# Attention, one-choice and two-choice expert layers in one launch on one core: hash rows finished in one step and moved by DMA, a cast moved to GpSimd, table fills laid out over the attention stage

## The chip, the cores and the metric

The kernel runs on one core of one Trainium2 chip. The metric is device microseconds of one execution. A core has five engines that run side by side, each with an instruction stream of its own, in order: PE (TensorE, matmul; its weight loads are shown as PEld), DVE (VectorE), ACT (ScalarE), POOL (GpSimd) and SP (SyncE), which here only issues DMAs. Sixteen DMA engines move the data. Whatever an engine waits for holds up everything behind it in its stream.

## The reference

```python
def reference(q, k, v, proj, moe, moe2):
    q_bits = einsum('bhsd,dk->bhsk', q, proj) > 0          # 6 bits a token
    k_bits = einsum('bhsd,dk->bhsk', k, proj) > 0
    mask = q_bucket[:, :, :, None] == k_bucket[:, :, None, :]   # all 6 bits equal
    scores = where(mask, q @ k.T / sqrt(64), -1e9)
    x = (softmax(scores) @ v)                              # 2 batches, 8 heads, 768 tokens, 64 wide
    x = x.transpose(0, 2, 1, 3).reshape(1536, 512)
    x = moe(x)     # the best of 8 experts a token, relu(x @ w1[e]) @ w2[e], times its weight
    return moe2(x) # the two best of 8 experts a token, noisy gate, the same kind of expert
```

## The kernel before

**Stages.** Attention comes first (to about 290 us), then the first expert layer (key 0 to 7), then the second (key 8 to 15). Attention has 16 heads (2 batches of 8) and works by groups: group g is half of head g // 2, so there are 32 groups of 384 queries. The two expert stages are planned apart from attention, in a second plan that the change does not touch.

**Precision.** Where f32 exactness is wanted, a value is split in a rounded high part and the rest (fp32r tiles: `hx` and `lx`, `eh` and `el`, two halves of `vh`), and matmuls are done on the parts.

**One head's preparation.** SP loads q and k of the head, turned, into `qk` (128 rows: 64 of q, 64 of k) and the values into `vr`. ACT rounds `qk` to `hx` (`prep_h`, L500); POOL subtracts to `lx` (`prep_l`, L544, four pieces). SP copies parts of `hx` and `lx` by DMA into `qa`, `ka`, `qb`, `kb` (`prep_hcopy` L508, four DMAs; `prep_lcopy` L548, two). `qa` and `ka` exist twice and alternate by head; `hx` has two buffers, so the rounding of head h waits until the DMAs that read `hx` of head h - 2 have landed.

**Hash rows.** PE projects `hx` and `lx` with the split `proj` (`bits_pe`, L567, into a PSUM tile `ET` of 108 rows, two pieces of 384 tokens). DVE makes the bits of it (`bits_sign`, L571): rows 64 to 75 of `qa` get the query's bits and the bits minus one, and rows 96 to 107 get the key's in the other order. Then the key's twelve rows are multiplied by 2^30 and moved down to rows 64 to 75 of `ka` (`bits_scale`): by DVE for heads 1 to 13 (L584, two pieces a head), by POOL for heads 14 and 15, by ACT for head 0 (`first_bits`, L538). Contracted together with the 64 rows of q and k they add minus 2^30 for each bit that differs, so the mask costs no pass of its own.

**One group.** PE makes three score pieces (`score_pe`, L597, four matmuls of 384 columns each, PSUM `S`, two buffers); DVE takes the row maximum (`score_max`, L602); POOL turns it into bias and scale, two small instructions (`score_scale`, L607 and L608); ACT takes the exponential into `es` (`score_exp`, L612). PE turns `es` in six blocks (`tr_pe`, L620, three transposes each, into `ET`, three buffers); ACT and DVE split each block (`tr_h` L624, `tr_l` L630); PE multiplies each block with the values, two matmuls (`pv`, L647 and L648, into `O`). The values' high part is a cast on DVE (`prep_vh`, L552), the low part two subtractions on POOL (`prep_vl`, L556). At a group's end ACT copies `O` out, PE turns it back (`fin_pe`, L657) and DVE scales it into `xrow` (`fin_out`, L671 and L673). So L671 runs once a group, and its start marks the end of that group.

**Order.** Each engine's order is made by a planner (`Plan`), from a cost and a due time for each step; `PR` is the table of due times. A planner's dependency only shapes the order: what an instruction really waits for on the chip follows from the data it reads and writes, and, for a DMA of SP, from the eighth DMA before it, which must have landed.

**Fills.** The gathered tables `xs1` and `xs2` and the output must hold a fill pattern before rows are scattered into them: 54 DMAs out of one row `zrow` (`init_x`, L454; with two small loads they are the list `inits`), some 260 KB each. SP issues them all in the first 135 us. After groups 14 and 15 the first six tiles of tokens are ranked, and POOL scatters their rows (`r1_scatter`, L719).

Of the kernel before, what the change touches and what calls it, by code (L numbers as in the profile page):

```python
# [9 lines left out]
F32 = mybir.dt.float32  # L10
F32R = mybir.dt.float32r
# [20 lines left out]
CB = float(2.0 ** 30)  # L32

# [4 lines left out]
PR = dict(sc=-7.0, mx=-7.5, ex=-5.5, pv=4.0, fin=7.0, bits=-16.0, prep=-26, load=-34.0, h=-1, l=0)  # L38
# [7 lines left out]
BSA, BSB, BSK, BSD, FSE = 1, 14, 2, .6, 0  # L46
BSE = lambda h: BSK if BSA <= h < BSB else 0
RA, K8, L1, L2 = 0, 7, 20, 1
WP, WR, WS = 4, 30, 2.5
LATE, ZP, Z2, L6, CR = 1, 23.0, 214.0, -4, 12  # L50
# [76 lines left out]
def fbits(t):  # L127
    return t.bitcast(F32)
# [3 lines left out]
def lsh_attention_moe_moe2_kernel(  # L132
# [251 lines left out]
    ld, wk, hl = ap("ld", 2), ap("wk", 2), ap("hl", 4)  # L384
# [26 lines left out]
    cbt = acon.tile([128, 192], F32, name="cbt")  # L411
    nc.gpsimd.memset(cbt[96:128], CB)

    def split_proj():
        nc.vector.tensor_copy(pst_h, pst)
        nc.vector.tensor_sub(pst_l, pst, pst_h)
# [119 lines left out]
    def first_bits(c):  # L536
        cs = slice(c * 384, c * 384 + 384)
        nc.scalar.activation(KA[0][64:76, cs], QA[0][96:108, cs], AF.Copy, scale=CB)  # L538
# [20 lines left out]
    BP = {}  # L559
# [9 lines left out]
    def bits_sign(h, c):  # L569
        cs = slice(c * 384, c * 384 + 384)  # L570
        nc.vector.tensor_scalar(QA[h % 2][64:108, cs], BP[h, c][64:108], 0.0, bsel[64:108],  # L571
                                op0=OP.is_gt, op1=OP.subtract)

    def bits_scale(h, c):
        s = h % 2
        if BSE(h) == 0:
            cs = slice(c * 192, c * 192 + 192)
            nc.gpsimd.tensor_tensor(KA[s][64:76, cs], QA[s][96:108, cs], cbt[96:108], op=OP.mult)
            return
        cs = slice(c * 384, c * 384 + 384)  # L580
# [7 lines left out]
    def score_pe(g, j):  # L588
        h, half = divmod(g, 2)
        s = h % 2  # L590
        if j == 0:
            SM[g] = wk.tile([128, 3], F32, name="sm", bufs=3)
        ES[g, j] = wk.tile([128, S], F32, name="es", bufs=8)
# [48 lines left out]
    def pv(g, kb):  # L642
        h = g // 2
        if kb == 0:
            OA[g] = psp.tile([128, 384], F32, name="O", bufs=1)
        w = VH[h][:, kb].rearrange("p a b -> p (a b)")
        nc.tensor.matmul(OA[g], w, EH[g, kb], start=kb == 0, stop=False)  # L647
        nc.tensor.matmul(OA[g], w, EL[g, kb], start=False, stop=kb == 5)  # L648
# [128 lines left out]
    plan = Plan(dict(S=2, ET=3, O=1, es=8, eh=4, el=4, ec=2, os=2, qk=3, vr=3, hx=2, lx=2, qb=2, vh=3,  # L777
# [8 lines left out]
    for h in range(HEADS):  # L786
        z = 12 * h
        due = lambda k, o=0.0: z + PR[k] + o
        if h > 1:
            add(("load", h), "SP", 1800, P(loads, h), due("load"), [("load", h - 1)] if h > 2 else [], lat=2200,  # L790
                new=[("qk", h), ("vr", h)])
# [27 lines left out]
        else:  # L819
            add(("ph", h), "ACT", 733, P(prep_h, h), due("prep"), ld_, use=[("qk", h)], new=[("hx", h)] + nq)  # L820
            add(("hc", h), "SP", 2500, P(prep_hcopy, h), due("prep", .1), [("ph", h)], lat=2200,
# [5 lines left out]
            add(("lc", h), "SP", 1250, P(prep_lcopy, h), due("prep", 1), [("pl", h, 3), ("hc", h)], lat=2200,  # L827
                use=[("lx", h), ("qb", h)])
            for c in range(2):
                add(("bp", h, c), "PE", 490, P(bits_pe, h, c), due("bits", 2 * c),  # L830
                    [("pl", h, 3), ("hc", h)], use=[("hx", h), ("lx", h)], new=[("ET", ("b", h, c))])
                add(("bt", h, c), "DVE", 525, P(bits_sign, h, c), due("bits", 2 * c + .5),
                    [("bp", h, c), ("hc", h)], use=[("ET", ("b", h, c)), ("qa", h)])
                for d in range(2):
                    if BSE(h) == 0:
                        add(("bs", h, 2 * c + d), "POOL", 552, P(bits_scale, h, 2 * c + d),
                            due("bits", 2 * c + .6 + .1 * d), [("bt", h, c)], use=[("qa", h)])
                    elif d == 0:
                        add(("bs", h, c), *(("ACT", 413) if BSE(h) == 1 else ("DVE", 269)), P(bits_scale, h, c),
                            due("bits", 2 * c + BSD), [("bt", h, c)], use=[("qa", h)])  # L840
        add(("vh", h), "DVE", 269, P(prep_vh, h), max(due("prep", 5), h - 5), ld_ + [("ph", h)] + FIRST[V0] * (h < 3) + [("at", 3 if h == 0 else 5)] * (h < 2), use=[("vr", h)],
# [5 lines left out]
    for g in range(NG):  # L847
        h = g // 2
        z = 6.0 * g
        for j in range(3):  # L850
            k, o = (g, j), 2 * j
            add(("sc",) + k, "PE", 650, P(score_pe, g, j), z + o + PR["sc"],
                ([("sc", g, j - 1)] if j else []) + (FIRST0[g] if h == 0 else [("hc", h)]) + [("lc", h)] + [("bt", h, c) for c in range(2)] + [("bs", h, c) for c in ((0, 3) if h == 0 else range(4) if BSE(h) == 0 else range(2))],
                use=[("qb", h), ("qa", h)] + ([("sm", g)] if j else []),
                new=[("S", k), ("es", k)] + ([] if j else [("sm", g)]))
            add(("mx",) + k, "DVE", 865, P(score_max, g, j), z + o + PR["mx"], [("sc",) + k], use=[("S", k)])
            add(("ms",) + k, *(("DVE", 135) if MS(g, j) else ("POOL", 330)), P(score_scale, g, j), z + o + PR["mx"] - 40, [("mx",) + k])
            add(("ex",) + k, "ACT", 971, P(score_exp, g, j), z + o + PR["ex"], [("ms",) + k],
                use=[("S", k), ("es", k), ("sm", g)])
        for kb in range(6):  # L860
            k = (g, kb)
            add(("tr",) + k, "PE", 330, P(tr_pe, g, kb), z + kb, [("ex", g, j) for j in range(3)] + [("c2",)],
                use=[("es", (g, j)) for j in range(3)], new=[("ET", k)])
            add(("th",) + k, "ACT", 371, P(tr_h, g, kb), z + kb + PR["h"], [("tr",) + k], use=[("ET", k)],
# [8 lines left out]
            else:  # L873
                add(("tl", 1) + k, "DVE", 469, P(tr_l, g, kb), z + kb + PR["l"], [("th",) + k],
                    use=[("ET", k), ("eh", k)], new=[("el", k)])
            add(("pv",) + k, "PE", 326, P(pv, g, kb), z + kb + PR["pv"],
                [("tl", 1) + k, ("vl", h, 1)] + ([("pv", g, kb - 1)] if kb else []),
                use=[("eh", k), ("el", k), ("vh", h)] + ([("O", g)] if kb else []), new=[] if kb else [("O", g)])
        add(("fa", g), "ACT", 371, P(fin_act, g), z + PR["fin"] - 1, [("pv", g, 5)], use=[("O", g)], new=[("os", g)])
        add(("fp", g), "PE", 598, P(fin_pe, g), z + PR["fin"], [("fa", g), ("ene",)], use=[("os", g)], new=[("ET", ("f", g))])  # L880
        add(("fs", g), *(("DVE", 70) if FSE else ("POOL", 190)), P(fin_eps, g), z + PR["fin"], [("ex", g, 2)], use=[("sm", g)])
        add(("fr", g), "DVE", 88, P(fin_rec, g), z + PR["fin"] - 1, [("fs", g)], use=[("sm", g)])
        add(("fo", g), "DVE", 363, P(fin_out, g), z + PR["fin"], [("fp", g), ("fr", g)],
            use=[("ET", ("f", g)), ("sm", g)])
    for k, f in enumerate(inits):
        add(("in", k), "SP", 900, f, 24 + 2.2 * k, [("in", k - 1)] if k else [("c3",), ("hc", 1)], lat=3000)
# [14 lines left out]
    for c in range(8):  # L901
        add(("wr", c), "SP", 1700, P(wload, c), (WR if c < WP else 150) + c, ([("in", 2)] if c < WP else [("in", len(inits) - 1)]) + ([("wl", c - 4, 7)] if c > 3 else []),
            lat=2500)
# [5 lines left out]
    for i, g in enumerate((14, 15, 30, 31)):  # L909
# [5 lines left out]
        for t in range(3):  # L915
            add(("rsa", T0, t), "ACT", 560, P(r1_sq, T0, t, 0), z - 3 + w * t, hot[:-1] + ([("rsa", T0, t - 1)] if t else []),
# [692 lines left out]
```

## Time and profile before

| what | value |
|---|---|
| three runs | 811.01, 807.99, 813.76 us, median 811.01 |
| the profiled execution: own time | 808.55 us |
| the profiled execution: span of its trace | 806.8 us |
| mean granted TensorE clock | 0.991 |
| PE busy | 774.3 us (96%) |
| DVE busy | 583.6 us (72%) |
| ACT busy | 479.5 us (59%) |
| POOL busy | 382.3 us (47%) |

The shares are averages over stages that have different limits. PE's busy time has matmuls that overlap: the duration of one is longer than the time from its start to the next one's. So pace is read from starts. Idle time of an engine stands in brackets, with what ended it.

### The profile page before, as it was taken

What the parts mean: (1) busy time and instruction counts of PE and PEld (TensorE: products, weight loads), DVE (VectorE), ACT (ScalarE), POOL (GpSimd) and SP (SyncE); (2) the same over time, 40 slices, a digit from 0 to 9 for tenths busy, and PEclk for the clock granted to TensorE, in tenths of its full rate; (3) what the DMA queues carried; (4) which work ended last, traced back from release to release, by engine and by line L of the source; (5) the groups of instructions that cost most, each with busy time, mean ns of one, the idle gap of its engine ahead of it and who ended that gap; (6) DMA issues with size and microseconds to landing.
All of it is one profiled execution on the core that took longest, in us unless ns stands there. A gap on an engine that the chain in (4) does not pass through costs nothing. (4 is left out here: it accounts for less than half of the span.)

```text
span 806.8 us, 14991 instructions
## 1 busy us (share of the span) xinstructions
PE 774.3 (96%) x5078; PEld 748.5 (93%) x5078; DVE 583.6 (72%) x1303; ACT 479.5 (59%) x1009; POOL 382.3 (47%) x669
## 2 busy tenths in 40 slices
PE   8999798998999999999999998999999999999995
PEld 6899787987999999999999998999999999999995
DVE  8999778999999868887787756684566475665511
ACT  6997777986888847556575544464353435354310
POOL 6655344557464260433123322108373745648474
PEclk9999989999999999999999999999999999999998
DMA  8999999664322158886677645765786776856332
GB/s 215 290 237 233 244 235 247 208 187 143 112 67 53 46 178 252 258 255 196 207 231 218 214 161 176 183 192 93 195 172 173 171 182 132 177 147 118 85 35 80
DMA packets 94076, 141.16 MB, mean 175 GB/s; under 512 B 26220, under 2 KB 58116, under 8 KB 93994
## 3 DMA queue, kind: packets, MB, share of 16 engines
q1 hardware_dynamic: 76730, 123.45, 55.2%
q0 software_dynamic: 17264, 16.70, 11.1%
q8 instruction: 42, 0.69, 0.4%
q14 instruction: 40, 0.33, 0.1%
HBM read 89.08 MB, written 36.06 MB: 155 GB/s over the span
## 5 line engine op out<-in xcount | busy, mean ns | idle before, releaser
L1264 POOL DMA_INDIRECT out_dram<-yo,idx x91 | 147.6, 1622 | 127.6 <-DVE yo L1261 102.0
L1056 PE MATMUL S<-xh,w0h 128*128 128x256 f32 (+1 forms) x512 | 165.0, 322 | 1.0 <-DVE hl L1066 1.0
L1057 PE MATMUL S<-xl,w0h 128*128 128x256 f32 (+1 forms) x512 | 161.4, 315 | 0.3 <-issue 0.3
L1058 PE MATMUL S<-xh,w0l 128*128 128x256 f32 (+1 forms) x512 | 161.7, 316 | 0.0
L1080 PE MATMUL ET<-hh,w1h 128*128 128x256 f32 (+2 forms) x504 | 158.5, 315 | 0.1
L1082 PE MATMUL ET<-hh,w1l 128*128 128x256 f32 (+2 forms) x504 | 158.2, 314 | 0.0
L1081 PE MATMUL ET<-hl,w1h 128*128 128x256 f32 (+2 forms) x504 | 157.8, 313 | 0.0
L1062 ACT ACTIVATE hh<-S 128x512 fp32r<-128x512 f32 (+1 forms) x64 | 46.8, 732 | 136.1 <-PE S L1058 130.1
L630 DVE TENSOR_TENSOR el<-ET,eh 128x384 fp32r<-128x384 f32 x192 | 102.0, 551 | 16.1 <-ACT eh L624 13.9
L612 ACT ACTIVATE es<-S,mxs 128x768 f32<-128x768 f32 x96 | 95.5, 995 | 15.7 <-POOL mxs L608 12.8
L620 PE MATMUL ET<-idf,es 128*128 128x128 f32 x576 | 92.1, 277 | 9.7 <-ACT es L612 7.1
L1066 DVE SCALAR_TENSOR_TENSOR hl<-S,hh 128x512 fp32r<-128x512 f32 (+1 forms) x64 | 54.5, 852 | 64.2 <-ACT hh L1062 62.3
L624 ACT ACTIVATE eh<-ET 128x384 fp32r<-128x384 f32 x192 | 89.7, 492 | 14.6 <-PE ET L620 11.3
L1056 PEld LDWEIGHTS S<-xh,w0h 128*128 128x128 f32 x512 | 96.3, 188 | 1.4 <-DVE hl L1066 1.2
L1057 PEld LDWEIGHTS S<-xl,w0h 128*128 128x128 f32 x512 | 96.4, 188 | 1.3 <-issue 0.5
L1058 PEld LDWEIGHTS S<-xh,w0l 128*128 128x128 f32 x512 | 96.2, 188 | 0.3
L1080 PEld LDWEIGHTS ET<-hh,w1h 128*128 128x128 f32 x504 | 94.9, 188 | 1.1 <-ACT ys L1104 0.7
L1081 PEld LDWEIGHTS ET<-hl,w1h 128*128 128x128 f32 x504 | 94.8, 188 | 0.7
L602 DVE TENSOR_REDUCE mxs<-S 128x1 f32<-128x768 f32 x96 | 91.5, 953 | 5.1 <-PE S L597 4.0
L1082 PEld LDWEIGHTS ET<-hh,w1l 128*128 128x128 f32 x504 | 94.7, 188 | 0.3
L620 PEld LDWEIGHTS ET<-idf,es 128*128 128x128 f32 x576 | 71.9, 142 | 20.6 <-ACT es L612 8.1
L217 DVE TENSOR_TENSOR w1l<-wraw,w1h 128x512 fp32r<-128x512 f32 x128 | 81.9, 681 | 11.8 <-ACT w1h L211 11.8
(257 smaller groups left out, 1474.7 us busy)
## 6 DMA issues: line engine op xcount, KB each, us to landing
wraw<-in_w1a_dram SPq DMA_DIRECT2D x32, 512.0 KB
wraw<-in_w2a_dram SPq DMA_DIRECT2D x32, 512.0 KB
wraw<-in_w1b_dram SPq DMA_DIRECT2D x32, 512.0 KB
wraw<-in_w2b_dram SPq DMA_DIRECT2D x32, 512.0 KB
xs<-zrow SPq DMA_DIRECT2D x26, 260.5 KB
xr<-xs SPq DMA_DIRECT2D x28, 208.0 KB
qk<-in_qk_dram SPq DMA_DIRECT2D x15, 384.0 KB
xs<-zrow SPq DMA_DIRECT2D x16, 261.0 KB
```

Of the source, the lines that this page charges most:

```text
L602: nc.vector.tensor_reduce(MX[(3 * g + j) % 9][:, 0:1], SC[g, j][:, :, :384], axis=AX.XY, op=OP.max, negate=True)
L612: nc.scalar.activation(ES[g, j].rearrange("p (a b) -> p a b", a=2), SC[g, j][:, :, :384], AF.Exp, bias=mx[:, 2:3], scale=mx[:, 1:2], accum ...
L620: nc.tensor.transpose(T[:, j * 128:j * 128 + 128], ES[g, j][:, kb * 128:kb * 128 + 128], idf)
L624: nc.scalar.activation(EH[g, kb], ET[g, kb], AF.Copy)
L630: nc.vector.tensor_tensor(EL[g, kb], ET[g, kb], EH[g, kb], op=OP.subtract)
L1056: nc.tensor.matmul(o, wH[n][:, fs], xh, start=kd == 0, stop=False)
L1057: nc.tensor.matmul(o, wH[n][:, fs], xl, start=False, stop=False)
L1058: nc.tensor.matmul(o, wL[n][:, fs], xh, start=False, stop=kd == 3)
L1080: nc.tensor.matmul(P, wH[n][:, ws], hh, start=f == 0, stop=False)
L1081: nc.tensor.matmul(P, wH[n][:, ws], hl_, start=False, stop=False)
L1082: nc.tensor.matmul(P, wL[n][:, ws], hh, start=False, stop=f == 7)
L1264: s = nc.gpsimd.indirect_dma_start(out=out.rearrange("n (a c) -> (n a) c", a=4), out_offset=bass.IndirectOffsetOnAxis(ap=IDX[e][:, b:b + 1 ...
```

## The change

Six things are changed, all in the attention stage.

1. The projection gets the sign of a column by one more DVE instruction at the start (`psg`), and `bits_sign` compares with one value a row and multiplies by another (1 or minus 2^30), so that the key's rows come out weighted. `bits_scale` goes; instead SP moves the twelve rows by one DMA a head, for heads 1 to 15 (`bits_copy`). Head 0 keeps its two ACT copies, without the factor.
2. The high part of the values is made by POOL.
3. The value product is planned two blocks a piece (`PVN`).
4. The fills get due times 3 apart and a dependency on the exponentials of a group, half a group further for each one; what follows them in the old plan now follows the fill that it needs.
5. `es` has 7 buffers for 8, `eh` and `el` 5 for 4; the squares of the last two rankings are due earlier (`RS`).
6. The planner's costs and the table of due times are new numbers, so that every engine's order is another one. In the expert stages the order of PE is the same instruction for instruction.

```diff
-PR = dict(sc=-7.0, mx=-7.5, ex=-5.5, pv=4.0, fin=7.0, bits=-16.0, prep=-26, load=-34.0, h=-1, l=0)
+PR = dict(sc=-5.4, mx=-8.7, ex=-5.34, pv=3.37, fin=3.38, bits=-14.64, prep=-18.57, load=-37.69, h=-17.66, l=0)
...
+    bthr = acon.tile([128, 1], F32, name="bthr")
+    nc.vector.tensor_scalar(bthr, bsel, -TINY, None, op0=OP.mult)
+    bval = acon.tile([128, 1], F32, name="bval")
+    nc.vector.memset(bval, 1.0)
+    nc.vector.memset(bval[96:128], -CB)
+    psg = acon.tile([128, 108], F32, name="psg")
+    nc.gpsimd.memset(psg, 1.0)
+    for c in (70, 96):
+        nc.gpsimd.memset(psg[:, c:c + 6], -1.0)
     def split_proj():
-        nc.vector.tensor_copy(pst_h, pst)
-        nc.vector.tensor_sub(pst_l, pst, pst_h)
+        nc.vector.tensor_tensor(psg, pst, psg, op=OP.mult)
+        nc.vector.tensor_copy(pst_h, psg)
+        nc.vector.tensor_sub(pst_l, psg, pst_h)
...
     def prep_vh(h):
         VH[h] = ld.tile([128, 6, 2, DH], F32R, name="vh", bufs=3)
-        nc.vector.tensor_copy(VH[h][:, :, 0, :], VR[h].rearrange("p (n d) -> p n d", d=DH))
+        nc.gpsimd.tensor_copy(VH[h][:, :, 0, :], VR[h].rearrange("p (n d) -> p n d", d=DH))
...
     def bits_sign(h, c):
         cs = slice(c * 384, c * 384 + 384)
-        nc.vector.tensor_scalar(QA[h % 2][64:108, cs], BP[h, c][64:108], 0.0, bsel[64:108],
-                                op0=OP.is_gt, op1=OP.subtract)
-
-    def bits_scale(h, c):
+        nc.vector.tensor_scalar(QA[h % 2][64:108, cs], BP[h, c][64:108], bthr[64:108], bval[64:108],
+                                op0=OP.is_gt, op1=OP.mult)
+
+    def bits_copy(h):
         s = h % 2
...
+        nc.sync.dma_start(fbits(KA[s][64:76]), fbits(QA[s][96:108]))
...
-    def pv(g, kb):
+    def pv(g, k0):
...
+        for kb in range(k0, k0 + PVN):
+            w = VH[h][:, kb].rearrange("p a b -> p (a b)")
+            nc.tensor.matmul(OA[g], w, EH[g, kb], start=kb == 0, stop=False)
+            nc.tensor.matmul(OA[g], w, EL[g, kb], start=False, stop=kb == 5)
...
     for k, f in enumerate(inits):
-        add(("in", k), "SP", 900, f, 24 + 2.2 * k, [("in", k - 1)] if k else [("c3",), ("hc", 1)], lat=3000)
+        add(("in", k), "SP", 900, f, 24 + 3 * k, [("in", k - 1), ("ex", int(3 + FILL * k), 0)] if k else [("c3",), ("hc", 1)], lat=3000)
```

SP, the copies of head 6 before (`qa` to `kb`) and what stands around them:

```order
L454 DMA out_dram<-zrow 16x8x512 x3
L454 DMA xs_59<-zrow 16x8x521 x6
L508 DMA qa_139<-hx 64x768
L508 DMA ka_140<-hx 64x768
L508 DMA qb<-hx 64x768
L508 DMA kb<-hx 64x768
L548 DMA qb<-lx 64x768
L548 DMA kb<-lx 64x768
L392 DMA qk<-in_qk_dram 128x768
L393 DMA vr<-in_v_dram 128x384
L454 DMA xs_59<-zrow 16x8x521 x10
```

SP, the same head's copies now; `ka<-qa` is the new DMA of the hash rows:

```order
L464 DMA xs_58<-zrow 16x8x522 x2
L518 DMA qa_146<-hx 64x768
L518 DMA ka_147<-hx 64x768
L518 DMA qb<-hx 64x768
L518 DMA kb<-hx 64x768
L558 DMA qb<-lx 64x768
L558 DMA kb<-lx 64x768
L393 DMA qk<-in_qk_dram 128x768
L394 DMA vr<-in_v_dram 128x384
L464 DMA xs_58<-zrow 16x8x522 x2
L586 DMA ka_147<-qa_146 12x768
```

Nine fills stood ahead of these copies and ten behind the next load; now two stand on either side, and so it goes on up to the last head.

DVE, the bits of head 8 before (`qa<-ET`, two pieces) with the scaling `ka<-qa` behind each:

```order
L571 TENSOR_SCALAR qa_139<-ET,bsel 44x384
L602 TENSOR_REDUCE mxs<-S 128x1
L671 TENSOR_TENSOR lgp<-ET,sm 128x24
L673 TENSOR_TENSOR xrow<-ET,sm 128x3x64
L584 TENSOR_SCALAR ka_140<-qa_139 12x384
L630 TENSOR_TENSOR el<-ET,eh 128x384
L571 TENSOR_SCALAR qa_139<-ET,bsel 44x384
L602 TENSOR_REDUCE mxs<-S 128x1
L630 TENSOR_TENSOR el<-ET,eh 128x384
L584 TENSOR_SCALAR ka_140<-qa_139 12x384
```

DVE, the same head now:

```order
L581 TENSOR_SCALAR qa_146<-ET,bthr,bval 44x384
L604 TENSOR_REDUCE mxs<-S 128x1
L632 TENSOR_TENSOR el<-ET,eh 128x384 x2
L581 TENSOR_SCALAR qa_146<-ET,bthr,bval 44x384
L667 RECIPROCAL sm<-sm 128x3
L604 TENSOR_REDUCE mxs<-S 128x1
L632 TENSOR_TENSOR el<-ET,eh 128x384 x3
L604 TENSOR_REDUCE mxs<-S 128x1
L674 TENSOR_TENSOR lgp<-ET,sm 128x24
L676 TENSOR_TENSOR xrow<-ET,sm 128x3x64
```

The two scalings and, further on, the cast of the values are gone from DVE's stream.

PE, from the end of head 8's second projection to its first score matmuls, now:

```order
L577 MATMUL ET<-lx,pst_h 108x384
...
L622 MATMUL ET<-idf,es 128x128 x3
L599 MATMUL S<-ka_150,qa_149 128x384 x2
L599 MATMUL S<-kb,qb 128x384 x2
L622 MATMUL ET<-idf,es 128x128 x6
...
L660 MATMUL ET<-selE,os 128x72 x3
L622 MATMUL ET<-idf,es 128x128 x6
...
L599 MATMUL S<-ka_147,qa_146 128x384 x2
```

In between, with the rows left out, PE has twelve matmuls of the value product in three pieces, two pieces of scores, six blocks of transposes and one turning back of `O`.

## Rows read from the trace of the kernel before

**Rows 1.** Busy time by stretch: stretch, sum, PE, PEld, DVE, ACT, POOL, clock, DMA.

```profile
60.00:80.00 20.00, 19.72 (x135) 18.57 (x133) 19.13 (x38) 16.48 (x39) 10.04 (x31) 1.00 0.99 234
80.00:100.00 20.00, 15.30 (x104) 14.17 (x102) 15.24 (x30) 13.74 (x31) 7.79 (x23) 0.99 0.97 237
100.00:120.00 20.00, 18.05 (x102) 16.71 (x102) 15.02 (x30) 14.64 (x36) 8.93 (x26) 0.84 0.98 235
...
180.00:200.00 20.00, 17.33 (x109) 14.80 (x108) 18.21 (x52) 12.69 (x27) 15.16 (x38) 1.00 0.53 166
...
240.00:260.00 20.00, 20.00 (x140) 19.54 (x139) 18.54 (x37) 17.08 (x37) 9.32 (x27) 1.00 0.24 61
```

**Rows 2.** Timeline of DVE, ends of groups 0, 6, 13, 24 and 28.

```profile
30.12 0.19 DVE L671 TENSOR_TENSOR lgp<-ET,sm 128x24 f32<-128x24 f32 x1
...
76.65 0.20 DVE L671 TENSOR_TENSOR lgp<-ET,sm 128x24 f32<-128x24 f32 x1
...
144.03 0.19 DVE L671 TENSOR_TENSOR lgp<-ET,sm 128x24 f32<-128x24 f32 x1
...
234.08 0.22 DVE L671 TENSOR_TENSOR lgp<-ET,sm 128x24 f32<-128x24 f32 x1
...
263.39 0.20 DVE L671 TENSOR_TENSOR lgp<-ET,sm 128x24 f32<-128x24 f32 x1
```

**Rows 3.** Timelines of PE and ACT, where PE stood longest.

```profile
100.45 0.47 PE L620 MATMUL ET<-idf,es 128*128 128x128 f32 x1 [3.81 <-ACT es L612]
98.58 0.84 ACT L500 ACTIVATE hx<-qk 128x768 fp32r<-128x768 f32 x1 [4.91 <-DMA kb<-hx]
```

**Rows 4.** Timeline of SP, 81 to 95 us: start, length, what is issued.

```profile
81.86 8.54 SPq L454 DMA_DIRECT2D xs<-zrow  x6
90.50 1.29 SPq L508 DMA_DIRECT2D qa<-hx  x1
...
94.21 0.60 SPq L508 DMA_DIRECT2D kb<-hx  x1
```

**Rows 5.** Waits from 0 to 210 us: total us, times, longest us.

```profile
ACT hx L500 <- DMA kb<-hx: 10.0, 3, 4.9
...
PE ET L620 <- DVE el L630: 1.7, 4, 1.0
```

**Rows 6.** Groups of instructions from 0 to 210 us: busy, mean ns, idle before.

```profile
L556 POOL TENSOR_TENSOR vh<-vr,vh 128x192 fp32r<-128x192 f32 x26 | 15.2, 608 | 5.7 <-DVE vh L552 5.5
...
L571 DVE TENSOR_SCALAR qa<-ET,bsel 44x384 fp32r<-44x384 f32 x26 | 16.2, 624 | 1.2 <-PE ET L567 0.4
...
L584 DVE TENSOR_SCALAR ka<-qa 12x384 fp32r<-12x384 f32 x24 | 10.0, 415 | 0.8
...
L552 DVE CAST vh<-vr 128x384 fp32r<-128x384 f32 x13 | 4.4, 347 | 0.0
```

**Rows 7.** Timeline of PE in an undisturbed stretch, 204.9 to 206.2 us.

```profile
204.91 0.82 PE L620 MATMUL ET<-idf,es 128*128 128x128 f32 x6
205.48 0.42 PE L647 MATMUL O<-eh,vh 128*128 128x384 f32 x1
205.74 0.34 PE L648 MATMUL O<-el,vh 128*128 128x384 f32 x1
205.92 0.49 PE L620 MATMUL ET<-idf,es 128*128 128x128 f32 x3
206.16 0.42 PE L647 MATMUL O<-eh,vh 128*128 128x384 f32 x1
```

**Rows 8.** Timelines of SP, DVE and POOL: two DMAs, issue and first use.

```profile
0.82 0.38 SPq L398 DMA_DIRECT2D wraw<-in_head_dram  x1
3.60 0.22 DVE L415 CAST pst_h<-wraw 128x108 fp32r<-128x108 f32 x1 [1.51 <-DMA wraw<-in_head_dram]
301.73 0.42 SPq L996 DMA_DIRECT2D meta<-xs  x1
308.98 0.36 POOL L1003 TENSOR_SCALAR va<-meta 128x2 f32<-128x2 f32 x1 [9.71 <-DMA meta<-xs]
```

More of the change, by code (lines that the diff above doesn't have):

```diff
@@ L789, in lsh_attention_moe_moe2_kernel @@
         if h > 1:
-            add(("load", h), "SP", 1800, P(loads, h), due("load"), [("load", h - 1)] if h > 2 else [], lat=2200,
+            add(("load", h), "SP", 1800, P(loads, h), due("load"), [("load", h - 1)] if h > 2 else [], lat=4500,
                 new=[("qk", h), ("vr", h)])
@@ L826, in lsh_attention_moe_moe2_kernel @@
                     use=[("qk", h), ("hx", h)] + ([("lx", h)] if c else []), new=[] if c else [("lx", h)])
-            add(("lc", h), "SP", 1250, P(prep_lcopy, h), due("prep", 1), [("pl", h, 3), ("hc", h)], lat=2200,
+            add(("lc", h), "SP", 1250, P(prep_lcopy, h), due("prep", 1), [("pl", h, 3), ("hc", h)], lat=3000,
                 use=[("lx", h), ("qb", h)])
             for c in range(2):
-                add(("bp", h, c), "PE", 490, P(bits_pe, h, c), due("bits", 2 * c),
+                add(("bp", h, c), "PE", 580, P(bits_pe, h, c), due("bits", 2 * c),
                     [("pl", h, 3), ("hc", h)], use=[("hx", h), ("lx", h)], new=[("ET", ("b", h, c))])
-                add(("bt", h, c), "DVE", 525, P(bits_sign, h, c), due("bits", 2 * c + .5),
+                add(("bt", h, c), "DVE", 640, P(bits_sign, h, c), due("bits", 2 * c + .5),
                     [("bp", h, c), ("hc", h)], use=[("ET", ("b", h, c)), ("qa", h)])
[L834 to L841, printed above, removed]
+            add(("bs", h, 0), "SP", 700, P(bits_copy, h), due("bits", 2.6), [("bt", h, 0), ("bt", h, 1)], lat=2800, use=[("qa", h)])
+        add(("vh", h), "POOL", 750, P(prep_vh, h), max(due("prep", 5), h - 5), ld_ + [("ph", h)] + FIRST[V0] * (h < 3) + [("at", 3 if h == 0 else 5)] * (h < 2), use=[("vr", h)],
             new=[("vh", h)])
@@ L851, in lsh_attention_moe_moe2_kernel @@
             k, o = (g, j), 2 * j
[L852 to L853 removed]
+            add(("sc",) + k, "PE", 770, P(score_pe, g, j), z + o + PR["sc"],
+                ([("sc", g, j - 1)] if j else []) + (FIRST0[g] if h == 0 else [("hc", h)]) + [("lc", h)] + [("bt", h, c) for c in range(2)] + [("bs", h, c) for c in ((0, 3) if h == 0 else (0,))],
                 use=[("qb", h), ("qa", h)] + ([("sm", g)] if j else []),
                 new=[("S", k), ("es", k)] + ([] if j else [("sm", g)]))
[L856 to L858 removed]
+            add(("mx",) + k, "DVE", 910, P(score_max, g, j), z + o + PR["mx"], [("sc",) + k], use=[("S", k)])
+            add(("ms",) + k, *(("DVE", 135) if MS(g, j) else ("POOL", 500)), P(score_scale, g, j), z + o + PR["mx"] - 40, [("mx",) + k])
+            add(("ex",) + k, "ACT", 1013, P(score_exp, g, j), z + o + PR["ex"], [("ms",) + k],
                 use=[("S", k), ("es", k), ("sm", g)])
@@ L861, in lsh_attention_moe_moe2_kernel @@
             k = (g, kb)
-            add(("tr",) + k, "PE", 330, P(tr_pe, g, kb), z + kb, [("ex", g, j) for j in range(3)] + [("c2",)],
+            add(("tr",) + k, "PE", 290, P(tr_pe, g, kb), z + kb, [("ex", g, j) for j in range(3)] + [("c2",)],
                 use=[("es", (g, j)) for j in range(3)], new=[("ET", k)])
-            add(("th",) + k, "ACT", 371, P(tr_h, g, kb), z + kb + PR["h"], [("tr",) + k], use=[("ET", k)],
+            add(("th",) + k, "ACT", 420, P(tr_h, g, kb), z + kb + PR["h"], [("tr",) + k], use=[("ET", k)],
                 new=[("eh", k)])
@@ L915, in lsh_attention_moe_moe2_kernel @@
         for t in range(3):
-            add(("rsa", T0, t), "ACT", 560, P(r1_sq, T0, t, 0), z - 3 + w * t, hot[:-1] + ([("rsa", T0, t - 1)] if t else []),
+            add(("rsa", T0, t), "ACT", 560, P(r1_sq, T0, t, 0), z - (3 if i < 2 else RS) + w * t, hot[:-1] + ([("rsa", T0, t - 1)] if t else []),
                 use=[("rt", T0)] if t else [], new=[] if t else [("rt", T0)])
```

57 lines of the change are left out of this document (23 added, 34 removed).

## The prediction

> **What bounds the kernel now.** I read the table of stretches first, for the stage with room. In the expert stages PE is full and its order does not change, so all of the change's effect has to come from attention. There the reader sees two kinds of stretch [rows 1]. At 240 to 260 us PE is busy all of 20 us, and DVE 18.54. At 80 to 100 PE falls to 15.30 us, with DVE, ACT and POOL all falling beside it: no engine is the bound there, so something outside of them is. The DMA column stands at 0.97 to 0.98, but it stands at 0.99 at 60 to 80 too, where PE still has 19.72. A full DMA alone is no stall.
>
> Next the ends of groups, which give the pace without any model of overlap [rows 2]. From group 24 to 28, 263.39 - 234.08 = 29.31 us for 4 groups, 7.33 each: the undisturbed pace. From 0 to 6, with DMAs full, 46.53 / 6 = 7.76. From 6 to 13, 67.38 / 7 = 9.63. From 13 to 24, 90.05 / 11 = 8.19.
>
> What sets 7.33? In an undisturbed stretch PE's matmuls start back to back [rows 7]: 0.18 us for 384 columns (205.74 to 205.92). With PE at 20.00 of 20 us [rows 1], PE is the floor of a group and DVE comes close behind.
>
> What makes 9.63? PE's longest stand, 3.81 us, ends with an exponential of ACT; ACT had itself stood 4.91 us for a buffer of `hx`, held by a DMA that reads it (`kb<-hx`) [rows 3]. That DMA was issued at 94.21, because the first of its four could only go at 90.50, behind six fills that took 8.54 us to issue [rows 4]. Over attention this wait of ACT is 10.0 us in 3 stands [rows 5]. The clock column confirms the cost: right after the stand the granted clock is 0.84 for 100 to 120 us instead of 1.00 [rows 1], so part of the stretch ran at the lower level of 1.2 GHz.
>
> **The change part by part.**
>
> *Fills laid out.* They go from nine or ten a row to two between one head's DMAs, so that the copies of a head never stand behind more than two. By 8.54 / 6 = 1.42 us a fill [rows 4] that is 2.8 us against some 13. ACT's stand and what it pulls along goes. What is late next is the pace with full DMAs, 7.76. So groups 6 to 13 give 7 x (9.63 - 7.76) = 13.1 us. The ends: 10.0, if only the stands of ACT themselves go [rows 5], and 7 x (9.63 - 7.33) = 16.1, if the stretch becomes undisturbed. I take -13.1, as the fills don't go away: 54 x 1.42 = 77 us of issue are spread over all heads, and the DMAs stay well used for longer.
>
> *DVE freed.* A head loses two scalings and a cast, 2 x 0.415 + 0.347 = 1.18 us [rows 6], 0.59 a group, for heads 1 to 13 (the others only the cast): some 16 us of DVE work. But PE is the floor, so only what PE waits for DVE is won: 1.7 us in 4 waits on `el` [rows 5]. The ends are 0 and the excess of all other groups over 7.33: 6 x 0.43 + 11 x 0.86 = 12.0. I take -1.7. In 180 to 200 POOL is at 15.16 us and PE at 17.33 [rows 1]; the scatters there are still POOL's in the new order, with score scaling queued behind them, so I expect that stand to stay.
>
> *The hash rows' DMA.* This is the added wait. Scaling on DVE took 0.415 us and was ready for PE at once; now SP must issue, and the twelve rows must land, before the head's first scores, and all of PE stands in line behind them. Between the second projection and those scores PE has work: 20 matmuls of 384 columns at 0.18, 3.6 us, and six blocks of transposes. A run of two blocks takes 0.57 and makes the matmul behind it 0.08 longer (0.26 against 0.18), a run of one 0.24 and 0.08 [rows 7]; two runs of each kind are 1.94. So 5.5 us, less 0.62 for the bits on DVE [rows 6]: 4.9 us are there for issue and landing. From below: the first load of the kernel came 2.8 us after its issue began (0.82 to 3.60) [rows 8]. In the middle: `kb<-hx`, at the end of a head's own copies, 94.21 to 98.58, 4.4 us [rows 3, 4]. From above: a small load behind weight loads, 301.73 to 308.98, 7.25 us [rows 8]. Most heads have nothing but two fills just ahead of it, and 4.4 fits in 4.9. In the new order three weight loads stand ahead of this DMA for heads 3 and 11, and a write of token rows for 9 and 10. At 7.25 each would lose 2.35 us, all four 9.4. I take one, +2.4; the ends are 0 and 9.4. On this the Trainium skill has a rule, "DMA: Bandwidth & Descriptors", section "Anatomy of one DMA": about 2 us a DMA are fixed, whatever its size, mostly until the write is confirmed. It speaks against moving 37 KB by DMA at all; the 2.8 us of the first load, with little queued ahead, agree in size. By the rule alone the copy would always be hidden, and the sum below would be lower by the 2.4 us; the 7.25 us show that what stands ahead in the queue matters more.
>
> *The values' cast on POOL.* Not seen before on POOL. From above by its two-input halves, 2 x 0.608 = 1.2 us [rows 6], from below by DVE's 0.347. POOL is busy half of a stretch [rows 1], and the low parts behind it are needed only by value products groups later: 0. If that cover fails, score scaling waits behind it, at worst 1.2 us a head, 19 us. If POOL were freed it could gain nothing that PE doesn't lose elsewhere, so the other end is 0.
>
> *Two blocks a piece.* PE switches less between transposes and products, but a switch is nearly free: two runs of one cost 2 x (0.24 + 0.08) = 0.64, one run of two 0.57 + 0.08 = 0.65 [rows 7]. 0, by either end. The matmuls are the same in number.
>
> *The start.* One more DVE instruction on the projection, of the size of the cast of 0.22 us [rows 8], ahead of the first projections: +0.2 (0 if the loads cover it). The buffers changed by one (`es`, `eh`, `el`), the earlier squares and the rest of the order: 0, within the 12.0 above on the good side; on the bad side they could cost what groups 0 to 6 show over the floor, 2.6.
>
> **The sum.** -13.1 - 1.7 + 2.4 + 0.2 = -12.2 us. The profiled execution took 808.55 us, 1.75 more than its span, and lies 2.46 under the median of the runs, 811.01. So it would become 796.4 and the median 798.8: I say 799.
>
> **The rivals.**
>
> *A: the gain is partly given back over the other heads.* The fills fill the DMAs also in groups 13 to 28, where they were out of the way. For: with full DMAs the pace was 7.76. Against: two fills a time, at most 2.8 us, and the other groups' DMAs were at 0.24 at 240 to 260 [rows 1]. Price: groups 24 to 28 and as many like them, 16 groups x 0.43 = 6.9, so 799 + 7 = 806.
>
> *B: more than I say.* With 0.59 us less a group DVE no longer comes close to the floor, and the new order follows measured durations; the groups outside of 6 to 13 fall toward 7.33. Price: the 12.0 above for the 1.7, of which I count the half and more, with 16.1 for 13.1: 811 - 16.1 - 8 + 2.6 = about 789.
>
> *C: the hash DMA is late for every head.* The place is the first score matmul of a head, and it decides as soon as issue and landing exceed 4.9 us. At 7.25 us each, 15 heads x 2.35 = 35.3 us against 13.1 + 1.7 = 14.8 won and 0.2 at the start: 811 + 35.3 - 14.6 = 832, slower than before. It is no gain already from about 5.9 us a head. For: the DMAs are shared with the head's own copies and the next load just before. Against: the copies are issued a group earlier, and 4.4 us were measured with full DMAs.
>
> *D: the fills were not the cause*, and the stretch at 80 to 140 stands for the copies' own bytes. Then about 811, no change. Against: at 60 to 80 the DMAs are as full, and PE is not held [rows 1].
>
> **How the numbers follow.** My forecast (793 to 803) 0.45; A (803 to 809) 0.23; B (under 793) 0.18; C and D together 0.14, C 0.08 of it. A measurement of this kernel tells about 1% from no change, 8 us: faster means under 803, slower over 819. Faster: 0.45 + 0.18 = 0.63, and a little for A's lower end: 0.64. Slower: C, 0.07 of its 0.08 beyond 819. Same: 0.29. The range takes A and most of B: 786 to 811; that leaves C, half of D and B's far end outside, and it is no wider than 16.1 + 12.0 down from the median (783) and D's 811 above.
>
> **What would show it.** Right: the ends of groups 6 to 13 at 7.4 to 7.9 us, no wait of ACT for `kb<-hx`, the clock at 1.00 all through attention, attention ending 11 to 13 us earlier and the expert stages as long as before. The hash DMA hidden: PE's waits at the score matmuls on ACT or PSUM only. Wrong: waits of PE at the score matmuls for the DMA `ka<-qa` in most heads (C), a pace of 7.8 or more in groups 13 to 28 with the DMA column over 0.8 (A), ACT waiting for POOL's scaling longer behind the new cast, or groups 6 to 13 still over 9 us (D).

## The result, and the profile after

| | before | changed |
|---|---|---|
| runs beside each other, median | 810.8 us (807.99 to 813.76) | 798.19 us (795.42 to 800.10) |
| ratio of the times | | 0.9837, interval 0.9804 to 0.9869 |
| profiled execution: own time, span | 808.55, 806.8 us | 797.71, 796.0 us |
| mean granted TensorE clock | 0.991 | 0.987 |
| PE, DVE, ACT, POOL busy | 774.3, 583.6, 479.5, 382.3 us | 768.9, 569.5, 476.9, 380.6 us |

Times are medians of the fast executions; of one trial below (the one with both kinds of DVE's work given back) that leaves out two of twelve, at 1071.27 and 1514.26 us, so that its median is 811.2 us and not 811.72.

The kernel became 1.6% faster, 12.6 us on the medians, against 12.2 predicted. The trace says from where. First the table of stretches of the changed kernel, in the columns of [rows 1]:

```profile
60.00:80.00 20.00, 20.00 (x139) 19.31 (x138) 18.77 (x35) 18.16 (x42) 12.32 (x36) 1.00 0.75 204
80.00:100.00 20.00, 20.00 (x139) 19.22 (x138) 18.34 (x36) 18.41 (x45) 13.45 (x39) 1.00 0.77 190
100.00:120.00 20.00, 20.00 (x140) 19.42 (x139) 18.71 (x37) 17.83 (x43) 10.30 (x33) 1.00 0.76 194
...
180.00:200.00 20.00, 18.57 (x127) 17.92 (x127) 16.75 (x32) 15.61 (x33) 7.52 (x24) 1.00 0.90 252
240.00:260.00 20.00, 18.80 (x132) 17.82 (x131) 15.95 (x41) 18.82 (x47) 4.55 (x18) 1.00 0.13 27
290.00:300.00 10.00, 8.08 (x50) 7.70 (x51) 7.42 (x16) 7.82 (x17) 1.46 (x3) 0.83 1.01 307
```

At 80 to 100 us PE went from 15.30 us and 104 matmuls to 20.00 and 139, and the granted clock of 100 to 120 from 0.84 to 1.00. At 240 to 260 it has less than before, 18.80 for 20.00. Only at the start was the clock lower than before, 0.66 for 1.00 from 10 to 20 us. The timeline of DVE gives the ends of groups 0, 6, 13, 24 and 31 (L674 is the old L671):

```profile
30.04 0.20 DVE L674 TENSOR_TENSOR lgp<-ET,sm 128x24 f32<-128x24 f32 x1
...
74.64 0.20 DVE L674 TENSOR_TENSOR lgp<-ET,sm 128x24 f32<-128x24 f32 x1
...
127.07 0.19 DVE L674 TENSOR_TENSOR lgp<-ET,sm 128x24 f32<-128x24 f32 x1
...
217.24 0.20 DVE L674 TENSOR_TENSOR lgp<-ET,sm 128x24 f32<-128x24 f32 x1
...
266.24 0.21 DVE L674 TENSOR_TENSOR lgp<-ET,sm 128x24 f32<-128x24 f32 x1
```

The differences of these ends, against those of before ([rows 2]; group 31 of before ended at 280.74), make the account. The last column is the span less the end of group 31; it holds the last ranking and both expert stages.

| us | to 0 | 0 to 6 | 6 to 13 | 13 to 24 | 24 to 31 | rest |
|---|---|---|---|---|---|---|
| before | 30.12 | 46.53 | 67.38 | 90.05 | 46.66 | 526.1 |
| changed | 30.04 | 44.60 | 52.43 | 90.17 | 49.00 | 529.8 |
| difference | -0.1 | -1.9 | -14.9 | +0.1 | +2.3 | +3.7 |

The sum is -10.8 us, the difference of the two spans. It is less than the 12.6 of the medians, because the profiled execution of before lay 2.25 us under its median and that of the changed kernel 0.48. All that was won lies in groups 0 to 13, 16.9 us, and 6 us of it are gone again by the end. The waits from 0 to 210 us (total us, times, longest):

```profile
POOL mxs L609 <- DVE mxs L604: 44.0, 38, 2.3
...
ACT es L614 <- POOL mxs L610: 12.4, 20, 1.6
DVE mxs L604 <- PE S L599: 9.9, 23, 2.1
```

ACT's 10.0 us for `kb<-hx` [rows 5] do not appear any more, and DVE now waits for PE's scores, 23 times. PE's floor set the pace up to group 12: that one ended at 119.25 us, and (119.25 - 30.04) / 12 = 7.43 us a group.

### The profile page after: what moved, and what is told of

Read it like the earlier page. It is cut to its first block, busy times and chain, and to the rows that moved or that the text cites. A ratio compares the mean times of both kernels' runs of the same rounds, so it can differ in the third digit from the quotient of the medians.

```text
span 796.0 us, 15061 instructions
## 1 busy us (share of the span) xinstructions
PE 768.9 (97%) x5078; PEld 747.7 (94%) x5078; DVE 569.5 (72%) x1265; ACT 476.9 (60%) x1009; POOL 380.6 (48%) x679
## 5 line engine op out<-in xcount | busy, mean ns | idle before, releaser
L632 DVE TENSOR_TENSOR el<-ET,eh 128x384 fp32r<-128x384 f32 x192 | 99.5, 550 | 6.8 <-ACT eh L626 4.0
L626 ACT ACTIVATE eh<-ET 128x384 fp32r<-128x384 f32 x192 | 87.1, 492 | 14.7 <-PE ET L622 13.8
L622 PE MATMUL ET<-idf,es 128*128 128x128 f32 x576 | 84.7, 273 | 0.6 <-DVE enT L501 0.4
L218 DVE TENSOR_TENSOR w0l<-wraw,w0h 128x512 fp32r<-128x512 f32 x120 | 76.3, 686 | 6.9 <-ACT w0h L212 6.8
```

The source lines that it names most:

```text
L218: eng.tensor_tensor(wL[n][:, c], wraw[n][:, c], wH[n][:, c], op=OP.subtract)
L626: nc.scalar.activation(EH[g, kb], ET[g, kb], AF.Copy)
L632: nc.vector.tensor_tensor(EL[g, kb], ET[g, kb], EH[g, kb], op=OP.subtract)
```

## The experiments

A ratio is to the kernel before on the same chip, whose median was 809.8 to 810.6 us. The changed kernel ran twice more for comparison; the first time:

> The changed kernel as it is, beside the next three on one chip: 796 to 800 us, 14 to 15 us earlier than before at the end of attention, some 4 us of it given back between the end of attention and the second expert.

Measured: 795.77 us, ratio 0.9832 (0.9811 to 0.9853), attention's end 265.18 us. The second time:

> The changed kernel once more, to compare the next two with on their own chip: about 797 us, the end of attention at 265 to 267 us.

Measured: 798.44 us, 0.9851 (0.9818 to 0.9884), attention's end 266.72 us. So three profiles of one kernel have spans of 793.9 to 797.1 us, with attention within 1.5 us.

**The fills alone**, in the kernel before. Four weight loads and the scatters, which the old plan put behind the last fill, follow fill 34 and fill 16 here, as in the changed kernel; these two lines are left out of the cut:

```diff
-        add(("in", k), ..., 24 + 2.2 * k, [("in", k - 1)] if k else ...)
+        add(("in", k), ..., 24 + 3 * k, [("in", k - 1), ("ex", int(3 + .5 * k), 0)] if k else ...)
```

> The kernel before, with the fills alone laid out over the groups (hash rows still scaled on DVE, cast still on DVE, old table of numbers). Theory, fills held ACT's rounding of hx and so PE: groups 6 to 13 fall from 9.6 us each to 7.4 to 7.8, the waits of ACT on kb<-hx go, and the time falls by 9 to 13 us (ratio 0.984 to 0.989). Rival, the freed DVE brought the gain: groups 6 to 13 stay over 9 us and the time moves by less than 3 us.

Measured: 802.72 us, 0.9896 (0.9854 to 0.9937). The ends of groups 6 and 13 in DVE's timeline:

```profile
77.37 0.21 DVE L671 TENSOR_TENSOR lgp<-ET,sm 128x24 f32<-128x24 f32 x1
...
132.58 0.20 DVE L671 TENSOR_TENSOR lgp<-ET,sm 128x24 f32<-128x24 f32 x1
```

That is 55.21 us for the seven groups, 12.2 less than before, by the fills' new places alone. The other groups are not faster (46.97 us from 0 to 6, 91.09 from 13 to 24, 46.67 from 24 to 31). The time fell by 7.9 us, less than the 9 to 13 expected: in the profile the rest took 531.9 us for 526.1. With DVE's work still there, a group takes 7.8 to 7.9 us, and PE now waits more for DVE than before. The waits on `el` from 0 to 210 us, of PE's weight loads and of its matmuls, before:

```profile
PEld ET L620 <- DVE el L630: 4.6, 10, 1.3
...
PE ET L620 <- DVE el L630: 1.7, 4, 1.0
```

and with the fills alone laid out:

```profile
PEld ET L620 <- DVE el L630: 7.5, 12, 0.9
...
PE ET L620 <- DVE el L630: 3.9, 9, 0.6
```

In the changed kernel 0.8 us of the weight loads' wait are left at these transposes, and none of the matmuls'.

**The rest of the change, with the fills bunched as before** (and the weight loads and scatters behind the last fill again):

```diff
-        add(("in", k), ..., 24 + 3 * k, [("in", k - 1), ("ex", int(3 + FILL * k), 0)] if k else ...)
+        add(("in", k), ..., 24 + 2.2 * k, [("in", k - 1)] if k else ...)
```

> The changed kernel with the fills bunched again as before; PE's and DVE's orders stay those of the changed kernel but for a few rows. Theory: groups 6 to 13 are over 9 us again and all the gain goes, 810 us or more; since the new DMA of the hash rows then stands behind eight fills a head (8 x 1.4 = 11 us of issue), it is late too, and the time may be up to 830. Rival, the freed DVE: within 3 us of the changed kernel's 798.

Measured: 819.65 us, 1.0105 (1.0056 to 1.0154), slower than before the change. SP's timeline, start and length of an issue:

```profile
100.03 9.79 SPq L464 DMA_DIRECT2D xs<-zrow  x8
109.92 1.31 SPq L586 DMA_DIRECT2D ka<-qa  x1
```

And PE's, three of the scores that come after such a DMA:

```profile
94.63 0.58 PE L599 MATMUL S<-ka,qa 96*128 96x384 f32 x2 [2.51 <-DMA ka<-qa]
...
114.06 0.59 PE L599 MATMUL S<-ka,qa 96*128 96x384 f32 x2 [2.71 <-issue]
...
133.54 0.89 PE L599 MATMUL S<-ka,qa 96*128 96x384 f32 x2 [4.27 <-issue]
```

The hash rows' DMA comes behind eight fills, and PE stands at the head's first scores. At 94.63 the profile names this DMA as what ended the wait; at the others it names nothing ("issue"), but they are the same place in the next two heads. From 6 to 13 a group takes 65.90 / 7 = 9.41 us. So a DMA on the path and bunched fills don't go together: the fills' edit is worth 8 us in the old kernel and 21 in the new one (819.65 against 798.19).

**DVE's two kinds of work given back, one at a time.** First the hash rows, copied by DVE in two pieces a head:

```diff
-        nc.sync.dma_start(fbits(KA[s][64:76]), fbits(QA[s][96:108]))
+        nc.vector.tensor_copy(KA[s][64:76, cs], QA[s][96:108, cs])
```

> The changed kernel with the hash rows of the key moved by DVE in two copies a head instead of by the DMA. Theory, PE is the floor at 7.4 us a group and the DMA is hidden: within 2 us of the changed kernel (796 to 800). Rival 1, DVE's time counts: 15 heads x 2 x 0.4 = 12 us slower. Rival 2, the DMA is late in some heads: up to 4 us faster than the changed kernel.

Then the cast of the values alone:

```diff
-        nc.gpsimd.tensor_copy(VH[h][:, :, 0, :], ...)
+        nc.vector.tensor_copy(VH[h][:, :, 0, :], ...)
```

> The changed kernel with the cast of the values on DVE again. Theory: within 2 us of the changed kernel. Rival 1, DVE's time counts: 16 x 0.35 = 5.6 us slower. Rival 2, the cast holds up POOL's score scaling: up to 16 x 0.5 = 8 us faster.

Measured: 805.25 us, 0.9933 (0.9906 to 0.9961), with the rows on DVE; 802.74 us, 0.9917 (0.9891 to 0.9943), with the cast. Each loses about half of what the whole change brings. The theory, within 2 us of the changed kernel, fell in both: they are 7.1 and 4.6 us slower, and the first rival is the nearer, that DVE's time counts. Both at once:

> The changed kernel with both parts of DVE's work given back: the key's hash rows copied by DVE in two pieces a head, and the values cast by DVE. What is left of the change is the fills, the pieces of two blocks and the planner's numbers. Theory (the freed work of DVE is worth what the two single trials showed, and they add): each group 7.43 + 0.22 + 0.11 = 7.76 us over the undisturbed groups, attention ending at 275 to 278 us, 806 to 810 us, so that fills alone under the old numbers were as good or better. Rival (DVE is the bound only in part, so that what the first part costs already holds the second): 7.65 a group and 804 to 806 us. Second rival (the new numbers carry a gain of their own): under 802.7, the time of the fills alone.

Measured: 811.2 us, 1.001 (0.9986 to 1.0034): nothing is left of the gain. Of the three expectations the first is the nearest (its range is passed by 1.2 us), the two costs add: 0.0096 and 0.0080 of ratio over the 0.9837 of the changed kernel make 1.001. The planner made each of these orders anew, from a table of due times that belongs to the changed kernel, so a part of the costs can be the order's. (The profiled execution was this kernel's fastest, 806.9 us, so its spans flatter it.) By stretches, as in the table above:

| us | to 0 | 0 to 6 | 6 to 13 | 13 to 24 | 24 to 31 | rest |
|---|---|---|---|---|---|---|
| fills alone | 30.40 | 46.97 | 55.21 | 91.09 | 46.67 | 531.9 |
| changed, both given back | 32.49 | 46.11 | 54.68 | 93.32 | 51.88 | 526.4 |

The stretch from 40 to 100 us of the version with both given back, in the columns of [rows 1]:

```profile
40.00:100.00 60.00, 59.91 (x401) 55.71 (x400) 57.71 (x114) 53.56 (x126) 33.38 (x97) 1.00 0.81 226
```

and of the changed kernel:

```profile
40.00:100.00 60.00, 60.00 (x414) 57.89 (x413) 55.80 (x105) 54.73 (x131) 36.57 (x107) 1.00 0.83 225
```

PE's busy share shows nothing, 59.91 against 60.00; its matmuls do: 401 against 414 in the same time, with DVE at 57.71 of 60. With the rows alone it is 402, with the cast alone 408, before the change 370. A busy PE is not PE at its peak, and the count tells it, as does the busy time of the weight loads, 55.71 us against 57.89.

**The value product one block a piece**, as it was before:

```diff
-FSE, PVN, HLN, ESN = 0, 2, 5, 7
+FSE, PVN, HLN, ESN = 0, 1, 5, 7
```

> The changed kernel with the value product planned one block a piece, as before. Theory (a switch between transposes and products costs nothing that can be measured, and the pieces don't matter): within 4 us of the changed kernel, 7.4 to 7.5 us a group. Rival (pieces of two keep PE's stream in longer runs and the split of a block off PE's path): 0.2 us a group more, 6 us in all, 803 or more.

Measured: 805.98 us, 0.9945 (0.9923 to 0.9967); the rival's number. The switches between transposes and other matmuls are about as many in the two traces, 280 for 282, if the turning back of `O` counts as a transpose; counted apart it is 284 for 254. So these runs don't show that switches cost nothing. From 40 to 100 us PE's weight loads have waits that the changed kernel does not have there, 1.1 us for exponentials and 0.8 for splits of DVE. The stretch:

```profile
40.00:100.00 60.00, 59.18 (x393) 54.52 (x392) 52.86 (x101) 53.82 (x128) 33.53 (x99) 1.00 0.79 216
```

393 matmuls against 414, with DVE at 52.86, so it is not DVE's load that bounds here. The next run asks whether it is the piece or its due time:

```diff
-PR = dict(..., pv=3.37, ...)
+PR = dict(..., pv=3.87, ...)
```

> The value product one block a piece, as in the run before, but each piece due half a block later, which is where a piece of two blocks had its blocks due on the mean. Theory (what the single blocks lost, about 8 us, comes from their place in PE's order: transposes were put close behind the exponentials that they need, with no product between; later pieces give the products back as filling): 798 to 801 us, the stretches at 40 to 100 us at 139 or 140 matmuls in 20 us as in the changed kernel. Rival (it is the length of a piece, whatever its due time): 804 us or more, 130 to 135 matmuls in 20 us as with one block.

Measured: 804.40 us, 0.9915 (0.9883 to 0.9947), 133 to 138 matmuls in 20 us from 40 to 100, attention's end 270.70 us instead of 279.45. In the trace the later due time gives back most; in the median 1.6 us, and the intervals overlap. By its number the rival is right, by its trace neither. So what a piece of two is worth apart from its due time stays open.

**Two places in which the gain is lost.** Group 17 ended 12.52 us after group 16, and three scatters stand on POOL there, two of them before the next score scaling. One trial puts scalings between them, with the orders of PE, DVE and ACT unchanged:

```diff
+                + ([("ms", 18 + 2 * i, t)] if i < 2 else [])
```

> The changed kernel with the scatters of the first six token tiles one by one, a score scaling of POOL between any two, instead of in pairs; the orders of PE, DVE and ACT stay as they are. Theory, the stop in groups 15 to 20 comes from score scaling behind a pair of scatters (2.6 us): 2 to 4 us faster. Rival, it comes from the ranking's block on DVE or the exponentials' order on ACT: within 1 us.

Measured: 800.30 us, 0.9872 (0.9851 to 0.9894), 4.5 us above the changed kernel's 795.77 on the same chip; group 17 still took 12.15 us, attention ended at 265.10. The scatters one behind the other are not what makes that group long. My theory fell, and what does is open. Nor is the time tied to that group: with the rows copied by DVE, group 17 took 7.13 us and group 19 took 12.03, and the eleven groups from 13 to 24 took 89.73 together, for 90.17.

The other place is the change from expert 0 to expert 1. Timeline of ACT, then of PE, in the changed kernel:

```profile
289.87 1.15 ACT L212 ACTIVATE w0h<-wraw 128x512 fp32r<-128x512 f32 x2 [5.01 <-DMA wraw<-in_w1a_dram]
```

```profile
291.43 0.73 PE L1124 MATMUL ET<-iw,ys 128*128 128x144 f32 x4 [1.50 <-ACT ys L1103]
...
292.65 0.39 PE L1079 MATMUL ET<-hh,w1h 128*128 128x256 f32 x1 [0.49 <-ACT ys L1103]
292.87 0.28 PE L1080 MATMUL ET<-hl,w1h 128*128 128x256 f32 x1
292.99 0.28 PE L1081 MATMUL ET<-hh,w1l 128*128 128x256 f32 x1
...
293.76 0.41 PE L1080 MATMUL ET<-hl,w1h 128*128 128x256 f32 x1
293.97 0.41 PE L1081 MATMUL ET<-hh,w1l 128*128 128x256 f32 x1
```

ACT stands 5.01 us for the weights of expert 1 with PE's next copy queued behind, PE stands 1.50 and 0.49, and then its matmuls start 0.21 us apart instead of 0.12: the stretch has the clock at 0.83. Before, PE had no such stand there. The trial issues these weight loads ahead of the scattered rows' reads:

```diff
-            add(("wr", n), ..., [("wr", n - 1) if n > 8 else ("xl", 1)] + ...)
+            add(("wr", n), ..., ([("wr", n - 1)] if n > 8 else []) + ...)
```

> The changed kernel with the first four weight loads of the second expert (expert 1) issued by SP ahead of the first reads of the scattered rows, not behind them. Theory, the 4 us given back come from these loads, which wait behind the scatter while PE is now earlier: ACT's wait of 5 us for them and PE's stop with the lower clock after it go, 2 to 4 us faster than the changed kernel. Rival: the rows of expert 1 now stand behind 2 MB of weights and are as late; no gain or up to 2 us slower.

Measured: 802.41 us, 0.9913 (0.9879 to 0.9946): 6.6 us slower than the changed kernel on the same chip, more than either expectation had. ACT now stood at the same place for the next loads:

```profile
291.85 0.63 ACT L212 ACTIVATE w1h<-wraw 128x512 fp32r<-128x512 f32 x1 [3.02 <-DMA wraw<-in_w2a_dram]
```

and PE 2.12 us behind it. Both edits together:

> Both of these edits: the two gains add, 4 to 8 us faster than the changed kernel, 790 to 794 us. Rival: what is won in attention is lost again at the start of the second expert, no more than the better of the two.

Measured: 802.74 us, 0.9896 (0.9872 to 0.9920), 7.0 us slower. In its profile the rest took 537.0 us, and PE stood 4.18 us for POOL at the end of expert 0. No version beat the changed kernel.

## Why the prediction was right, and where its sum was not

The time came out at 798.19 us for 799, and the end of attention 14.5 us earlier for 11 to 13. But two terms were off, in opposite directions, one cost was missed, and one zero was none.

**Fills laid out, -13.1: right in groups 6 to 13.** Alone they gave -12.2 us there (the median of the whole kernel fell by 7.9), at 55.21 / 7 = 7.89 us a group for the 7.76 that I took as what comes next. The 10.0 of ACT's stands alone would have been too little. Rival D (the fills are not the cause) is out, by 8 us in the median.

**DVE freed, -1.7: mis-sized.** The step that failed is "PE is the floor, so only what PE waits for DVE is won". Groups 24 to 28 showed the floor; in most of attention PE was not at it. The 1.7 us were the waits of the matmuls alone, where the weight loads had 4.6; and they were read from a trace in which the fills held all engines up. With the fills out of the way the same two rows are 3.9 and 7.5 us. Over the fills alone the changed kernel won 46.97 - 44.60 = 2.4 us in groups 0 to 6 and 55.21 - 52.43 = 2.8 in 6 to 13, 5.2 us together.

Given back within the changed kernel, the work costs 12.8 us (811.2 against 798.44 on the same chip), more than the 12.0 that I had as its end; in the profiles 3.8 us lie in groups 0 to 13, 2.4 ahead of them and 6.0 behind them up to group 31, while the stages after that were 3.3 shorter. How much of it is the order's is not separated. So this is rival B's mechanism, DVE that came close to the floor, in groups 0 to 13. B's place was too wide: from 13 to 24 nothing was won against before (90.17 for 90.05). What holds these groups I did not find; that the scatters stand one behind the other is not it.

**The hash rows' DMA, +2.4: mis-sized, it cost nothing.** In PE's timeline the first scores of head 6 follow back to back, with no wait:

```profile
98.16 0.49 PE L622 MATMUL ET<-idf,es 128*128 128x128 f32 x3
98.40 0.60 PE L599 MATMUL S<-ka,qa 96*128 96x384 f32 x2
```

and SP had issued that head's DMA at 93.99:

```profile
87.88 1.23 SPq L464 DMA_DIRECT2D xs<-zrow  x2
93.99 0.80 SPq L586 DMA_DIRECT2D ka<-qa  x1
```

So 4.41 us were enough, where I had 4.9 as the time that is there; in twelve of the fifteen heads it was 4.4 to 4.5, in one 4.02, in two over 6, and PE has no wait at these scores that this DMA ended. The 4.9 was near by two errors: PE has 6.2 us of work there (92.21 to 98.40), because I left out the turning back of `O`, 0.72; and the bits are ready not 0.62 but 1.8 us after the projection (at 93.97), because DVE does two pieces of `el` first. The landing itself is best read where PE did wait, in the run with bunched fills: 3.9 to 4.2 us from the start of the issue. So the margin was some 0.2 to 0.5 us. SP was through with the two fills 4.9 us before it. The slow case that I took one of, 7.25 us behind weight loads, did not show; rival C fell. Its condition is real, though: with the fills bunched PE stood three times between 80 and 150 us, 2.5 to 4.3 us each, at such scores. The Trainium skill, "DMA: Bandwidth & Descriptors", section "Anatomy of one DMA", has about 2 us fixed for a DMA of any size, given there for DMAs that GpSimd issues, while this one is SP's, which the prediction did not say; by that rule the copy is always hidden, as it was here, and not where the issue itself came late.

**The cast on POOL, 0: right.** It takes POOL 0.50 us a head, between the bounds of 0.347 and 1.2 (from 0 to 210 us):

```profile
L562 POOL CAST vh<-vr 128x384 fp32r<-128x384 f32 x15 | 7.5, 504 | 0.1
```

and no wait of PE on `vh` shows. ACT's waits for POOL's score scaling are 12.4 us, before 12.8. Given back to DVE it cost 0.0080 of ratio.

**Two blocks a piece, 0: wrong as an edit by itself.** The step was "a switch is nearly free", and no run tests it by itself; but I looked for no other effect. Undone alone it costs 7.8 us (805.98). Since the table of due times was made for pieces of two, part of this belongs to the table.

**The rest of the order, 0, and the start, +0.2.** The first group ended as before (30.04 for 30.12), although the sign "the clock at 1.00 all through attention" did not hold there (0.66 from 10 to 20 us). But the new order (table, costs, buffers, pieces of two) is not neutral: with DVE's work back it eats the 8 us that the fills alone give (811.2 against 802.72). It pays because DVE is free; the terms of my sum don't add up one by one.

**What I missed.** "The expert stages as long as before" is wrong: the rest took 529.8 us for 526.1 (528.7 and 530.4 in the two later profiles), and groups 24 to 31 took 2.3 us more. The second is the new order's and not the fills': with the fills alone these groups took 46.67 us, as before (46.66). For the first, the trace shows the stand of ACT and PE between the first two experts. PE came to the second product of expert 0 16.7 us earlier than before, the load that it needs next only 14.1 (ACT's first rounding of it started at 289.87 for 303.93). The one cure that I tried moved the stand to the next loads. The stand is not all of the 3.7 us. PE's first matmuls of expert 0's second product and of expert 1, before:

```profile
300.76 0.28 PE L1080 MATMUL ET<-hh,w1h 128*128 128x256 f32 x1
...
314.06 0.37 PE L1056 MATMUL S<-xh,w0h 128*128 128x256 f32 x1
```

and in the changed kernel:

```profile
284.07 0.28 PE L1079 MATMUL ET<-hh,w1h 128*128 128x256 f32 x1
...
301.11 0.37 PE L1055 MATMUL S<-xh,w0h 128*128 128x256 f32 x1
```

The stretch with the stand is 17.04 us for 13.30, 3.7 more; but from the end of group 31 to its start it is 17.83 for 20.02, 2.2 less. So about 1.5 us of the 3.7 lie ahead of expert 1, and about 2.2 behind. Behind, at the change from the first expert layer to the second, the granted clock was 0.77 from 480 to 495 us, and before 0.83 from 495 to 505; as time lost that is 3.4 us for 1.7, an estimate (0.23 of 15 us, 0.17 of 10). One of the later profiles of the changed kernel had 0.89 and the other 0.77, so whether the longer stretch belongs to the change is not shown with one profile of before. Over all profiles the rest varied from 526 to 537 us, with PE's order there the same.

Rival A had its gain given back over the other heads through the DMAs; these stayed well used (0.90 at 180 to 200), but groups 13 to 24 did not get longer, so the place and the cause are others. Its sign, a pace of 7.8 us or more in groups 13 to 28, could not tell: that pace was 8.08 us (group 28 ended at 248.28), but 7.96 before.

Together: -13.1 and -1.7 predicted for groups 0 to 13, -16.9 measured; +2.4 and +0.2 predicted, 0 measured; nothing predicted behind group 13, +6.1 measured. The sum was right because a gain too small and a cost too large stood against a loss that I had not seen. That the number came within 1 us is luck; that laying out the fills would bring most of it is not.

## What to carry to other kernels

Long runs of filler DMAs in a queue that also carries copies on the path are worth spreading out, and more so when another copy moves to that queue: here 8 us became 21. Where PE looks full, count its matmuls per stretch before calling it the floor, since an engine close behind it takes a few per cent that the waits of the matmuls hardly name (those of the weight loads name some). A wait that is read from a trace in which something else holds all engines up can grow once that is gone: here 1.7 us became 3.9. When edits come with an order planned for them, undo them singly and together: here DVE's two added up, but their common base was worth nothing without them.

## What the runs showed of the hardware

- A DMA of twelve rows (36 KB) was used 4.0 to 4.5 us after its issue began without any wait in thirteen heads, with the sixteen DMA engines 0.50 to 0.72 busy from the issue to the use. Behind eight fills, at a share of 0.84, PE had its rows 114.06 - 109.92 = 4.1 us after the issue began, and in the next head, at 0.89, 133.54 - 129.60 = 3.9. So the engines' load mattered little; when SP got to issue mattered.
- The issue of a fill took mostly 0.6 to 0.75 us in a run of two (1.23 / 2 above) and 9.79 / 8 = 1.22 us in a run of eight, near the 1.42 of [rows 4]. What makes it longer in a long run is not shown.
- After stands of 1.50 and 0.49 us PE went on for some matmuls at 0.12 us a start and then fell to 0.21, with the granted clock of the stretch at 0.83: part of it ran at 1.2 GHz instead of 2.4. Waits of 1.0 to 1.4 us within attention left the clock at 1.00 (140 to 200 us).
